# A second Strassen level inside one product of a cross network, with one-bank PSUM tiles and hand-set engine orders, on one NeuronCore

## The chip, the cores and the metric

The kernel runs on one NeuronCore of a Trainium2 chip. The metric is the device time of one execution in microseconds (us), as a median of several runs. A profile is one execution; its span is some 1.7 us shorter than the time reported for the same run. Engines are named as in the profile: PE is TensorE's matmuls, PEld its weight loads, DVE is VectorE, ACT is ScalarE, POOL is GpSimd, SP issues the transfers.

## The reference

```python
B, Din, L = 16384, 1024, 6          # x0 [B, Din], ws [L, Din, Din], bs [L, Din], all bf16
def reference(x0, ws, bs):
    x = x0
    for l in range(L):
        proj = jnp.einsum('bd,de->be', x, ws[l]) + bs[l]
        x = x0 * proj + x
    return x
```

## The kernel before

The batch is cut into 16 pairs of two blocks of 512 rows. A pair goes through 6 layers, so the program is 96 layers one after the other, each needing the result of the one before. Activations lie transposed, `[128, 2, 8, 512]`.

A layer is a 2x2 block product, done with seven products in place of eight (Strassen's scheme in Winograd's form). Each product is 16 matmuls of 128x512. Three things surround the products: VectorE builds four operand differences T1 to T4; ScalarE evicts PSUM (the memory in which TensorE's results land) to bf16 tiles in SBUF, the memory that VectorE works in; VectorE adds the parts, multiplies by x0 and adds x, which gives the next layer's input. Four of the seven weight operands are sums of weight blocks ("combinations"). They are the same for every pair, so VectorE builds those of layer l+1 while pair 0 runs layer l, saves them to DRAM (`Lc`), and later pairs load them.

```python
def emit_T(xsrc, which):                       # T1 = B12-B11, T2 = B22-T1, T3 = B22-B12, T4 = B21-T2
    ...
            nc.vector.tensor_tensor(out=t_[:], in0=B12, in1=B11, op=SUB)
def emit_combo(l, pid):                        # pair 0 only; 5: W12+W22, 6: c5-W11, 3: W21-c6, 7: W11-W12
    ...
    pending_saves.append((l, pid, t_))
def product(pid, pts, start):                  # 16 matmuls into two 2-bank PSUM tiles
    for m in range(KH):
        for k in range(KH):
            nc.tensor.matmul(pts[m // 2][:, m % 2, :], lhsT=wt[:, k, m * P:(m + 1) * P], rhs=rhs[:, k, :], ...)
...
product(1, pA, True);  P1s = evac(pA)
product(5, pX, True);  P5s = evac(pX)
product(3, pX, False); S53 = evac(pX, bias_eh=0)
product(2, pX2, True); P2s = evac(pX2, bias_eh=0)       # product 2 is W21*B21
nc.vector.tensor_tensor(out=C1[:, :, 0, :], in0=P1s, in1=P2s, op=ADD)
final(C1, 0, 0)                                         # c *= x0; x_next = c + x
if combos_next:
    emit_combo(l + 1, 5)
product(6, pA, False); ...; emit_combo(l + 1, 6)
product(7, pA, False); ...; emit_combo(l + 1, 3)
product(4, pA, False); ...; emit_combo(l + 1, 7)
```

A scheduler decides each engine's order within the data dependences.

## Time and profile before

| | before |
|---|---|
| time, median | 2353.59 us (three runs, 2353.52 to 2353.95) |
| PE, DVE, ACT busy | 98%, 73%, 66% of 2352.8 us |
| one steady layer on PE | 24.17 us |
| first matmul starts | 12.63 us |
| from the end of the last layer on PE to the end | 16.0 us |

Two lines of the page of before: the busy time of each engine, and the shares of the chain of work that ended last.

```profile
PE 2312.4 (98%) x10537; PEld 1052.7 (45%) x10752; DVE 1708.6 (73%) x1464; ACT 1556.7 (66%) x2113; POOL 1.2 (0%) x5
...
PE 96%; DVE 1%; DMA 1%; issue 1%; SPq 1%; ACT 0%; another core or an unknown queue 0%; DVEq 0%
```

TensorE is the bound. The next lines are the timeline of PE in before: start, duration, and a run of equal matmuls. Two products that open a layer are shown; no idle time is printed before either.

```profile
1031.43 3.62 PE L196 MATMUL pa<-x0T,wp 128*128 128x512 bf16 x16
...
1055.60 3.62 PE L196 MATMUL pa<-xst,wp 128*128 128x512 bf16 x16
```

The starts are 24.17 us apart for 112 matmuls, 215.8 ns each. (A few matmul records are missing from such traces; the starts are what to use.)

The windows view gives the busy time of each engine in a stretch, here one stretch for each of a few layers of before and one for the end.

```profile
core 0: us, PE busy (x) PEld busy (x) DVE busy (x) ACT busy (x) POOL busy (x), PEclk, DMA share, GB/s
12.63:39.44 26.81, 26.70 (x111) 11.57 (x113) 15.82 (x14) 14.94 (x20) 0.96 (x1) 1.00 0.80 263
39.44:64.05 24.61, 24.22 (x111) 10.97 (x112) 21.78 (x20) 16.21 (x22) 0.00 (x0) 1.00 0.48 156
...
1079.78:1103.95 24.17, 24.07 (x112) 10.97 (x113) 17.56 (x16) 16.20 (x22) 0.00 (x0) 1.00 0.76 263
...
2336.80:2352.80 16.00, 0.15 (x1) 0.00 (x0) 4.50 (x4) 1.27 (x2) 0.00 (x0) 0.57 0.91 227
```

(The DMA share can pass 1.00.) In an ordinary layer (third line) VectorE is busy 17.6 of 24.17 us. In pair 0 it also builds combinations and is busy 21.8 (second line), still less than PE. The last line is the end: VectorE works 4.5 us after the last matmul, then transposes and stores follow.

This is the timeline of DVE in before.

```profile
1046.74 1.22 DVE L235 TENSOR_TENSOR cb<-ev 128x2048 bf16<-128x2048 bf16 x1 [7.94 <-ACT ev L208]
1048.00 1.22 DVE L214 TENSOR_TENSOR cb<-cb,x0T 128x2048 bf16<-128x2048 bf16 x1
1049.26 1.22 DVE L223 TENSOR_TENSOR xst<-cb,x0T 128x2048 bf16<-128x2048 bf16 x1
1050.40 1.22 DVE L241 TENSOR_TENSOR cb<-ev 128x2048 bf16<-128x2048 bf16 x1
```

Each takes 1.22 us. One that needs the result of the one before starts 1.26 us after it; an independent one 1.14 us after it. The bracket on the first line is a wait of 7.94 us, nearly all of VectorE's spare time in that layer.

### The profile page before, as it was taken

Reading aid. Unit: us, or ns where it says so; the run is one execution under the profiler, and the core shown is the slowest. Engines: PE = TensorE matmul, PEld = TensorE weight load, DVE = VectorE, ACT = ScalarE, POOL = GpSimd, SP = SyncE. Lnnn points to the kernel's source line nnn. Section 1 sums busy time; section 2 is a strip of 40 time slices with the busy share of each in tenths; the row PEclk is TensorE's granted clock in tenths of the full one; section 3 lists DMA queues with packets and bytes.
Section 4 is the critical chain, followed back from the end, with each engine's and each line's share of the span. In section 5 each row is a group of like instructions: output and inputs, shape, how many; then the busy total and the mean of one; then the engine's idle time right before and its main releaser. Section 6 shows DMA issues by size and latency. Waiting matters only on the chain.

```text
span 2352.8 us, 27562 instructions
## 1 busy us (share of the span) xinstructions
PE 2312.4 (98%) x10537; PEld 1052.7 (45%) x10752; DVE 1708.6 (73%) x1464; ACT 1556.7 (66%) x2113; POOL 1.2 (0%) x5
## 2 busy tenths in 40 slices
PE   7999999999999999999999999999999999999997
PEld 3444444444444444444444444444444444444443
DVE  5977767676777767676776767677776767777675
ACT  4666666666666666666666666666666666666665
POOL 0000000000000000000000000000000000000000
PEclk9999999999999999999999999999999999999998
DMA  7769485584956849568494774947749476594843
GB/s 226 203 210 256 152 216 196 161 253 154 228 184 171 241 154 240 171 177 235 153 259 153 178 233 152 259 152 190 221 152 260 153 198 214 155 257 152 226 153 86
DMA packets 599987, 457.96 MB, mean 195 GB/s; under 512 B 398128, under 2 KB 550704, under 8 KB 599856
## 3 DMA queue, kind: packets, MB, share of 16 engines
q1 hardware_dynamic: 599856, 456.20, 67.0%
q8 instruction: 85, 1.39, 0.2%
q14 instruction: 46, 0.38, 0.1%
HBM read 342.88 MB, written 46.14 MB: 165 GB/s over the span
## 4 chain that ended last, share of the span: by engine, by line
PE 96%; DVE 1%; DMA 1%; issue 1%; SPq 1%; ACT 0%; another core or an unknown queue 0%; DVEq 0%
PE pa L196 54%; PE px L196 42%; SPq L145 1%; DMA w_313<-in_ws_dram 0%; DMA wp<-in_ws_dram 0%; DVE cb L214 0%; DVE xst L219 0%; DVE xst L223 0%; ACT ev L208 0%; DVE cb L241 0%; DVE cb L250 0%; DVE cb L235 0%; DVE wp L128 0%; DVE T_247 L93 0%; DVE T_811 L93 0%
## 5 line engine op out<-in xcount | busy, mean ns | idle before, releaser
L196 PEld LDWEIGHTS <-wp 128*128 128x128 bf16 x10752 | 1052.7, 98 | 1283.8 <-issue 12.7
L208 ACT ACTIVATE ev<-px,b_all 128x512 bf16<-128x512 f32 x768 | 486.3, 684 | 201.3 <-PE px L196 193.3
L196 PE MATMUL px<-xst,wp 128*128 128x512 bf16 x2510 | 562.5, 379 | 2.7
L235 DVE TENSOR_TENSOR cb<-ev 128x2048 bf16<-128x2048 bf16 x96 | 117.6, 1225 | 594.2 <-ACT ev L208 594.2
L205 ACT CAST ev<-pa 128x1024 bf16<-128x1024 f32 x384 | 388.6, 1012 | 240.2 <-PE pa L196 230.8
L214 DVE TENSOR_TENSOR cb<-cb,x0T 128x2048 bf16<-128x2048 bf16 x384 | 467.8, 1221 | 6.3
L223 DVE TENSOR_TENSOR xst<-cb,xst 128x2048 bf16<-128x2048 bf16 x316 | 385.0, 1222 | 14.5
L208 ACT ACTIVATE ev<-pa,b_all 128x512 bf16<-128x512 f32 x384 | 243.1, 684 | 112.9 <-PE pa L196 108.2
L208 ACT ACTIVATE cb<-pa,b_all 128x512 bf16<-128x512 f32 x384 | 243.1, 684 | 88.4 <-ACT ev L208 48.4
L196 PE MATMUL pa<-xst,wp 128*128 128x512 bf16 x1254 | 287.3, 379 | 1.3
L205 ACT CAST ev<-px 128x1024 bf16<-128x1024 f32 x192 | 194.3, 1012 | 138.1 <-PE px L196 133.1
L241 DVE TENSOR_TENSOR cb<-ev 128x2048 bf16<-128x2048 bf16 x96 | 117.0, 1219 | 0.0
L250 DVE TENSOR_TENSOR cb<-ev 128x2048 bf16<-128x2048 bf16 x96 | 117.0, 1218 | 0.0
L196 PE MATMUL px<-x0T,wp 128*128 128x512 bf16 x501 | 112.4, 379 | 0.5
L223 DVE TENSOR_TENSOR xst<-cb,x0T 128x2048 bf16<-128x2048 bf16 x64 | 78.3, 1223 | 1.5
L196 PE MATMUL pa<-x0T,wp 128*128 128x512 bf16 x251 | 60.2, 391 | 12.9 <-DMA x0T<-in_x_dram 12.6
L130 DVE TENSOR_TENSOR wp<-wp 128x2048 bf16<-128x2048 bf16 x6 | 7.3, 1219 | 2.1 <-DMA wp<-in_ws_dram 2.1
L128 DVE TENSOR_TENSOR wp<-wp 128x2048 bf16<-128x2048 bf16 x6 | 7.3, 1219 | 0.0
L126 DVE TENSOR_TENSOR wp<-w_90,wp 128x2048 bf16<-128x2048 bf16 x1 | 1.2, 1226 | 8.2 <-DMA wp<-in_ws_dram 8.2
L93 DVE TENSOR_TENSOR T_111<-x0T 128x2048 bf16<-128x2048 bf16 x1 | 1.2, 1226 | 5.7 <-DMA x0T<-in_x_dram 5.7
L219 DVE TENSOR_TENSOR xst<-cb,xst 128x2048 bf16<-128x2048 bf16 x4 | 4.9, 1225 | 0.1
L196 PE MATMUL px<-T_247,wp 128*128 128x512 bf16 x16 | 3.6, 378 | 0.3 <-DVE T_247 L93 0.3
(783 smaller groups left out, 1858.9 us busy)
## 6 DMA issues: line engine op xcount, KB each, us to landing
wp<-Lc SPq DMA_DIRECT2D x360, 512.0 KB, 3.4
wp<-in_ws_dram SPq DMA_DIRECT2D x288, 512.0 KB, 3.7
out_dram<-x0T SPq DMA_DIRECT2D x30, 1024.0 KB, 9.8
Lc<-wp SPq DMA_DIRECT2D x24, 512.0 KB, 3.1
out_dram<-xoS SPq DMA_DIRECT2D x4, 512.0 KB, 4.7
w_90<-in_ws_dram SPq DMA_DIRECT2D x1, 512.0 KB, 4.7
x0T<-in_x_dram SPq DMA_TRANSPOSE x32, 7.3
w_130<-in_ws_dram SPq DMA_DIRECT2D x1, 512.0 KB, 5.0
```

What stands on the lines that cost most here:

```text
L128: nc.vector.tensor_tensor(out=t_[:], in0=wtiles[(0, l, 5)][:], in1=W11[:], op=SUB)
L130: nc.vector.tensor_tensor(out=t_[:], in0=W21[:], in1=wtiles[(0, l, 6)][:], op=SUB)
L145: nc.sync.dma_start_transpose(out=x0T_next[:, n], in_=x0[n * NB:(n + 1) * NB, :])
L196: nc.tensor.matmul(pts[m // 2][:, m % 2, :], lhsT=wt[:, k, m * P:(m + 1) * P], rhs=rhs[:, k, :], start=(start and k == 0), stop=(k == KH - ...
L205: nc.scalar.copy(out=dst[:, 2 * h:2 * h + 2, :], in_=pts[h][:])
L208: nc.scalar.activation(out=dst[:, m, :], in_=pts[m // 2][:, m % 2, :], func=IDENT, bias=bias_col(bias_eh, m), scale=1.0)
L214: nc.vector.tensor_tensor(out=c, in0=c, in1=blk(x0T, eh, n), op=MULT)
L219: nc.vector.tensor_tensor(out=xo_last["xfin"][:, eh, n].rearrange("r j k p -> r k j p"), in0=v4(c), in1=v4(blk(xsrc, eh, n)), op=ADD)
L223: nc.vector.tensor_tensor(out=blk(xst, eh, n), in0=c, in1=blk(xsrc, eh, n), op=ADD)
L235: nc.vector.tensor_tensor(out=C1[:, :, 0, :], in0=P1s, in1=P2s, op=ADD)
L241: nc.vector.tensor_tensor(out=C1[:, :, 1, :], in0=U2s, in1=S53, op=ADD)
L250: nc.vector.tensor_tensor(out=C2[:, :, 1, :], in0=U3s, in1=P5s, op=ADD)
```

## The change

The intent is to apply the same scheme once more to one of the seven products, W21*B21 (product 2), so that its 16 matmuls of 128x512 become 7 inner products of four matmuls of 128x256, the work of 14. That needs four inner operands (`emit_t`), three inner sums of 128x512 on VectorE, and a fifth combination per layer, "2i". PSUM tiles become single banks, evicted one by one. The program order is declared binding for TensorE, ScalarE and VectorE. All five combinations of the next layer are now emitted together, in front of the first inner sum. The diff, cut to its core:

```diff
-    psA = ctx.enter_context(tc.tile_pool(name="psA", bufs=2, space=bass.MemoryType.PSUM))
...
+    wring = ctx.enter_context(tc.tile_pool(name="wring", bufs=14))
+    psum = ctx.enter_context(tc.tile_pool(name="ps", bufs=1, space=bass.MemoryType.PSUM))
+    pA = [psum.tile([P, NB], FP32, name=f"pA{i}") for i in range(KH)]
+    pX = [psum.tile([P, NB], FP32, name=f"pX{i}") for i in range(KH)]
+    def emit_t(B):                            # inner operands of 128x512
+        tt(t1, q(0, 1), q(0, 0), SUB); tt(t2, q(1, 1), t1, SUB)      # (joined here)
+        tt(t3, q(1, 1), q(0, 1), SUB); tt(t4, q(1, 0), t2, SUB)
...
+            s = inner_w(t_)                   # the fifth combination, "2i"
+            tt(s[5], a21, a22, ADD)
+            tt(s[6], s[5], a11, SUB)
+            tt(s[3], a12, s[6], SUB)
+            tt(s[7], a11, a21, SUB)
...
+    order_ctx = ctx.enter_context(tc.manual_schedule(engines={nc.tensor.engine, nc.scalar.engine, nc.vector.engine}))
...
     prefetch_upto(PREF)
     flush_saves()
...
+            if combos_next:
+                for pid in (5, 6, 3, "2i", 7):
+                    emit_combo(l + 1, pid)
+            inner(1, 0, True)
+            ev(i15[:, 0, :], pX[0][:])
+            inner(5, 1, True)
+            ...
+            inner(2, 2, True)
+            ev(i2[:], pX[2][:])
+            tt(cq(0, 0), q3(i15[:, 0, :]), q3(i2[:]), ADD)
+            ...                               # groups of products 6 and 7 between inner 6, 3, 7, 4
+            tt(Q2[:], Q2[:], P1s[:], ADD)
+            final(Q2[:], 0, 0)
+            final(U2s[:], 0, 1, mult=False)
+            if not last_layer:
+                emit_T(xst, Tn, (1,))
+            ...                               # rest of product 7, then product 4
+            final(C21[:], 1, 0)
+            if not last_layer:
+                ti_next = emit_t(blk(xst, 1, 0))
+                emit_T(xst, Tn, (2, 3, 4))
```

## The prediction

> **What bounds the kernel now.** TensorE. The page's busy table has PE 98% of 2352.8 us, VectorE (DVE) 73%, ScalarE (ACT) 66%; the chain that ended last is 96% PE. In the timeline 16 matmuls of 128x512 start every 3.4525 us, 215.8 ns each, so a layer's 112 take 24.17 us, and 96 layers 2320 us. The rest, 33 us, is the start (first matmul at 12.6 us, then cold ones, about 3.7 us lost) and the end (about 16 us after the last matmul).
>
> **Per layer.**
> - PE: one 16-matmul product (W21*B21) becomes seven inner products of four 128x256 matmuls. The Trainium skill (TensorE: Matmul & The Clock Gate, "Back-to-back issue gap") gives N/2.4 + 2.5 ns; that agrees with the 215.8 ns here and gives 109.2 ns for N=256, an estimate; the trace of before has no such matmul. 96 x 215.8 + 28 x 109.5 ns = 23.78 us, saving 0.39 us a layer, 37 us in all (1.6%). The weight loads (98 ns in the page) must hide behind 107 ns; I expect they just do.
> - DVE: 15 full 128x2048 ops stay (1.22 us; start to start 1.14 us independent, 1.26 us dependent, from the timeline). Added are 4 inner operand subtractions and 3 inner sums of 128x512, about 0.42 us each (estimate: same slope, and the fixed part of about 150 cycles of VectorE: DVE Perf Modes, "Side-by-side"). DVE goes from about 17.1 to 21 of 23.8 us.
> - ACT: 31 evictions of one bank instead of 22; biased 0.684 us as before, plain about 0.585 us (estimate from 1.012 us for 1024 columns). About 19 us of 23.8: not binding; its one-bank tiles come free before PE needs them.
> - DMA: one weight more per layer, share about 67% to 74%. Not binding.
>
> **Steady layers (pairs 1 to 15).** I added these durations along the fixed orders. The last inner product ends about 18.6 us after the layer's start; its eviction and three dependent DVE ops give the next layer's first operand about 0.3 us before PE asks for it; T2 for product 6 comes equally tight. So PE stays gapless at 23.78 us, but without reserve.
>
> **Pair 0.** DVE also builds next-layer weight combinations, five now, all put before the first inner sum: 4 x 1.2 + 4 x 0.4 us, so DVE needs 27 us per layer and becomes the bound: 26.98 us in layers 1 to 4. In layer 0 they also wait for W22 of layer 1, whose load now stands behind five saves in the queue: about 6 us lost. Together about 19 us of the 37 are given back.
>
> **End.** The last region follows the last product at once; perhaps 1.5 us saved.
>
> **Sum.** 2353.6 - 37 + 19 - 1.5, about 2334 us. Range 2318 to 2350. Chances: faster by over 2% 0.03, within 2% 0.92, slower by over 2% 0.05.
>
> **What would show it.** Windows of 23.78 us per layer in later pairs; 128x256 matmuls 109 to 110 ns apart; PE waits on DVE tiles (xst, T) of about 3 us per layer in pair 0, longest in layer 0 after a DVE wait for weight DMA; DVE busy 86 to 90%; small DVE ops 0.42 us.
>
> **What would make it wrong.** Weight loads not hidden behind 107 ns of streaming: 5 ns per small matmul is 13 us. The eviction-to-sum chain longer than I added up: stalls in every layer, and 0.25 us each cancels the rest of the gain. Small DVE ops nearer 0.5 us: pair 0 and the layer boundaries slip. Combinations fitting into DVE idle time better than I think: towards 2315 us. Weight transfers late at pair boundaries, where DMA is already saturated.

## The result

| | before | after |
|---|---|---|
| median | 2353.69 us | 2344.47 us |
| range | 2353.52 to 2353.95 (4 runs) | 2342.43 to 2346.23 (4 runs) |
| ratio, 95% interval | | 0.996 (0.9946 to 0.9974) |

A ratio is the mean time of one kernel's runs over the mean of the other's in the same rounds, so it is not quite the ratio of the medians. The kernel gains 9.2 us, clear of noise; 19.6 were forecast. The result passed the comparison with the reference.

The same two lines of the page, after.

```profile
PE 2277.5 (97%) x11668; PEld 1164.1 (50%) x11904; DVE 2003.2 (86%) x2160; ACT 1818.9 (78%) x2977; POOL 1.1 (0%) x5
...
PE 87%; DVE 10%; issue 1%; ACT 1%; SPq 1%; DMA 0%; DVEq 0%
```

VectorE has gone from 1% to 10% of the chain that ended last. First a steady stretch, the timeline of PE after: the openings of two layers, and a pair of inner products between them.

```profile
1015.86 1.03 PE L233 MATMUL pA_88<-xst,wp 128*128 128x512 bf16 x4
...
1026.22 0.60 PE L245 MATMUL pX_92<-xst,wp 128*128 128x256 bf16 x4
1026.66 0.60 PE L245 MATMUL pX_93<-ti,wp 128*128 128x256 bf16 x4
...
1039.64 1.03 PE L233 MATMUL pA_88<-x0T,wp 128*128 128x512 bf16 x4
```

The steady layer is 23.78 us, as forecast, and the four small matmuls take 0.44 us. The layer's total says it more exactly: (23.78 us - 96 x 215.8 ns) / 28 = 109 ns each. The weight loads hide. So the loss is not in the steady layers. The windows view after, layer by layer (layers 0, 1, 2 and 5 of pair 0, then a steady layer, the last layer, and the end):

```profile
core 0: us, PE busy (x) PEld busy (x) DVE busy (x) ACT busy (x) POOL busy (x), PEclk, DMA share, GB/s
11.80:49.19 37.39, 26.00 (x123) 12.55 (x125) 24.62 (x32) 19.49 (x32) 0.94 (x1) 0.88 0.90 282
49.19:76.25 27.06, 26.01 (x122) 12.55 (x125) 26.51 (x31) 18.94 (x31) 0.00 (x0) 0.92 0.52 181
76.25:103.46 27.21, 23.78 (x121) 12.05 (x125) 26.52 (x31) 18.94 (x31) 0.00 (x0) 1.00 0.54 151
158.22:183.68 25.46, 25.36 (x122) 12.50 (x125) 23.18 (x28) 18.23 (x30) 0.00 (x0) 0.93 0.57 198
...
1063.42:1087.20 23.78, 23.62 (x123) 12.11 (x125) 20.48 (x23) 18.94 (x32) 0.00 (x0) 1.00 1.12 237
2300.32:2324.10 23.78, 23.62 (x122) 12.02 (x123) 20.62 (x23) 18.95 (x32) 0.00 (x0) 1.00 0.01 1
2324.10:2342.70 18.60, 0.16 (x1) 0.00 (x0) 6.78 (x6) 0.71 (x2) 0.00 (x0) 0.58 0.94 226
```

Compare VectorE (the third busy figure) with the length of the stretch. In the steady layer it is busy 20.5 of 23.78 us. In layers 1 and 2 it is busy 26.5 of 27.1: it is full, and TensorE waits for it. Layer 0 is 11.4 us longer than TensorE is busy in it (37.39 against 26.00), and the end is 18.6 us where it was 16.0.

The differences of the two profiles add up to the whole gain (10.1 us between these two executions, 9.2 between the medians):

| stretch | before | after | difference |
|---|---|---|---|
| up to the first matmul | 12.63 | 11.80 | -0.8 |
| six layers of pair 0 | 148.6 | 171.9 | +23.3 |
| the other 90 layers | 2175.6 | 2140.4 | -35.2 |
| end | 16.0 | 18.6 | +2.6 |
| span | 2352.8 | 2342.7 | -10.1 |

So the second level gains 35 us in pairs 1 to 15, and two thirds of that are given back in pair 0. The six layers there took 37.39, 27.06, 27.21, 27.20, 27.56 and 25.46 us. Against TensorE's own work (23.78 us a layer, plus the 3.5 us that before loses there too, most of it in its first 16 matmuls, which took 6.25 us where later ones took 3.62: 148.6 - 6 x 24.17) that is a loss of 25.7 us: 10.1, 3.3, 3.4, 3.4, 3.8 and 1.7.

The loss in layer 0 shows in VectorE's timeline after: the operation at 26.61 is the last of the set-up, the one at 35.33 the first combination of layer 1.

```profile
26.61 1.22 DVE L91 TENSOR_TENSOR T_137<-x0T,T_131 128x2048 bf16<-128x2048 bf16 x1
35.33 1.23 DVE L91 TENSOR_TENSOR wp<-w_151,wp 128x2048 bf16<-128x2048 bf16 x1 [7.50 <-DMA wp<-in_ws_dram]
36.59 4.07 DVE L91 TENSOR_TENSOR wp<-wp 128x2048 bf16<-128x2048 bf16 x6
```

It waits 7.50 us for a weight block, and everything behind it in the binding order waits as well, the first inner sum included. The transfer queue of after says why the block is late: five saves, which need VectorE's own results, are issued before the loads of W21 and W22.

```profile
17.12 9.92 SPq L126 DMA_DIRECT2D Lc<-wp  x5
27.10 1.34 SPq L83 DMA_DIRECT2D wp<-in_ws_dram  x2
```

Before had this order in its queue too (four saves, then the two loads at 22.49), but there VectorE used W22 only at 32.98, behind work of the layer itself.

On TensorE (timeline after) the openings of the next layers wait for `xst`, VectorE's output:

```profile
49.19 1.87 PE L233 MATMUL pA_88<-xst,wp 128*128 128x512 bf16 x4 [11.28 <-DVE xst L91]
...
76.25 1.02 PE L233 MATMUL pA_88<-xst,wp 128*128 128x512 bf16 x4 [0.95 <-DVE xst L91]
...
103.46 1.02 PE L233 MATMUL pA_88<-xst,wp 128*128 128x512 bf16 x4 [3.27 <-DVE xst L91]
```

The first four matmuls after the 11.28 us of waiting take 1.87 us, the next openings 1.02. The windows view of after around the opening of layer 1 and of layer 5, the PEclk column:

```profile
49.20:52.60 3.40, 3.40 (x9) 1.17 (x10) 3.34 (x3) 0.69 (x1) 0.00 (x0) 0.50 0.68 255
158.22:161.60 3.38, 3.38 (x11) 1.31 (x12) 3.35 (x3) 1.37 (x2) 0.00 (x0) 0.68 1.05 405
```

The clock was 0.50 after 11.28 us of idle time and 0.68 after 3.62 us, as a mean of 3.38 us (in the first 0.98 of these it was still 1.00, in the next 3.30 it was 0.54); after 3.27 us (layers 3 and 4) it stayed at 1.00. In layer 1 this costs nothing, because VectorE is the bound there: the layer takes 27.06 us, layer 2 with the clock at 1.00 takes 27.21. In layer 5, where VectorE has no combinations to build, it makes 1.7 us. The Trainium skill (TensorE: Matmul & The Clock Gate, "The HAM clock gate") has the clock fall to a half after an idle window of about 3.4 us. The half (0.50) agrees, but the length is no sharp limit in these runs: in the run loads_first, told below, the clock fell after 2.89 us before layer 1 (0.50) and after 3.28 us before layer 3 (0.54).

### The profile page after: what moved, and what is told of

Read it like the earlier page. It is cut to its first block, busy times and chain, and to the rows that moved or that the text cites. A ratio compares the mean times of both kernels' runs of the same rounds, so it can differ in the third digit from the quotient of the medians.

```text
span 2342.7 us, 31963 instructions
## 1 busy us (share of the span) xinstructions
PE 2277.5 (97%) x11668; PEld 1164.1 (50%) x11904; DVE 2003.2 (86%) x2160; ACT 1818.9 (78%) x2977; POOL 1.1 (0%) x5
## 4 chain that ended last, share of the span: by engine, by line
PE 87%; DVE 10%; issue 1%; ACT 1%; SPq 1%; DMA 0%; DVEq 0%
PE pA_91 L233 13%; PE pA_88 L233 13%; PE pA_89 L233 13%; PE pA_90 L233 12%; PE pX_92 L245 7%; PE pX_94 L233 6%; PE pX_93 L233 6%; PE pX_95 L233 6%; PE pX_92 L233 6%; DVE ev L91 4%; PE pX_93 L245 3%; DVE xst L91 2%; PE pX_94 L245 2%; DVE wp L91 1%; DVE ti L91 1%
## 5 line engine op out<-in xcount | busy, mean ns | idle before, releaser
L233 PEld LDWEIGHTS <-wp 128*128 128x128 bf16 x9216 | 901.4, 98 | 1026.5 <-issue 55.1
L91 DVE TENSOR_TENSOR ev<-ev,x0T 128x2048 bf16<-128x2048 bf16 x384 | 469.8, 1223 | 9.9
L91 DVE TENSOR_TENSOR xst<-ev,xst 128x2048 bf16<-128x2048 bf16 x320 | 384.9, 1224 | 21.7 <-DVE ev L91 0.5
L91 DVE TENSOR_TENSOR ev<-ev 128x2048 bf16<-128x2048 bf16 x288 | 352.2, 1223 | 38.0 <-ACT ev L249 25.7
L245 PEld LDWEIGHTS <-wp 128*128 128x128 bf16 x2688 | 262.7, 98 | 133.2
L252 ACT ACTIVATE ev<-pA_88,b_all 128x512 bf16<-128x512 f32 x288 | 198.4, 689 | 69.9 <-PE pA_88 L233 65.7
L252 ACT ACTIVATE ev<-pA_90,b_all 128x512 bf16<-128x512 f32 x288 | 198.1, 688 | 34.9 <-PE pA_90 L233 33.4
L252 ACT ACTIVATE ev<-pA_91,b_all 128x512 bf16<-128x512 f32 x288 | 197.9, 687 | 34.0 <-PE pA_91 L233 34.0
L252 ACT ACTIVATE ev<-pA_89,b_all 128x512 bf16<-128x512 f32 x288 | 198.3, 689 | 25.6 <-PE pA_89 L233 1.8
L245 PE MATMUL pX_92<-ti,wp 128*128 128x256 bf16 x1152 | 172.8, 273 | 1.1
L249 ACT CAST ev<-pX_92 128x512 bf16<-128x512 f32 x192 | 112.3, 585 | 28.8 <-PE pX_92 L233 16.7
L233 PE MATMUL pA_88<-xst,wp 128*128 128x512 bf16 x320 | 83.0, 382 | 22.4 <-DVE xst L91 22.4
L252 ACT ACTIVATE ev<-pX_92,b_all 128x512 bf16<-128x512 f32 x96 | 66.0, 687 | 26.6 <-PE pX_92 L233 24.3
L233 PE MATMUL pA_89<-xst,wp 128*128 128x512 bf16 x314 | 83.2, 385 | 0.3
L233 PE MATMUL pA_91<-xst,wp 128*128 128x512 bf16 x315 | 82.3, 381 | 0.6
L233 PE MATMUL pX_94<-xst,wp 128*128 128x512 bf16 x320 | 82.1, 379 | 0.3
L233 PE MATMUL pA_90<-xst,wp 128*128 128x512 bf16 x306 | 81.7, 385 | 0.4
L233 PE MATMUL pX_93<-xst,wp 128*128 128x512 bf16 x308 | 80.5, 379 | 0.7
L233 PE MATMUL pX_95<-xst,wp 128*128 128x512 bf16 x308 | 80.5, 379 | 0.3
L233 PE MATMUL pX_92<-xst,wp 128*128 128x512 bf16 x306 | 80.3, 379 | 0.4
L252 ACT ACTIVATE ev<-pX_93,b_all 128x512 bf16<-128x512 f32 x96 | 66.0, 687 | 16.9 <-PE pX_93 L233 15.7
L252 ACT ACTIVATE ev<-pX_94,b_all 128x512 bf16<-128x512 f32 x96 | 66.0, 687 | 16.9 <-PE pX_94 L233 16.9
```

Of the source, the lines that this page charges most:

```text
L91: nc.vector.tensor_tensor(out=out, in0=in0, in1=in1, op=op)
L233: nc.tensor.matmul(dst[m][:], lhsT=wt[:, k, m * P:(m + 1) * P], rhs=rhs[:, k, :], start=(start and k == 0), stop=(k == KH - 1), skip_group ...
L245: nc.tensor.matmul(dst[:, m * NQ:(m + 1) * NQ], lhsT=wv[:, k, m * P:(m + 1) * P], rhs=ti[i][:, k, :], start=(start and m == 0 and k == 0), ...
L249: nc.scalar.copy(out=dst, in_=src)
L252: nc.scalar.activation(out=dst, in_=src, func=IDENT, bias=bias_col(eh, m), scale=1.0)
```

## The experiments

Theory A: what stretches pair 0 is the volume of VectorE's work, about 27 us a layer once it also builds five combinations, and in layer 0 the wait for W22 behind the saves. Theory B: the place of the combinations in front of the first inner sum delays the chain. Theory C: the inner products, evictions or transfers themselves are slower than thought. Eight kernels were run, five rounds each, in two calls; the runs of before there gave 2354.08 and 2353.88 us.

| run | median us | ratio to before (95%) | result |
|---|---|---|---|
| after | 2344.47 | 0.996 (0.9946 to 0.9974) | correct |
| loads_first | 2337.2 | 0.9929 (0.9915 to 0.9942) | correct |
| spread | 2339.93 | 0.994 (0.9927 to 0.9952) | correct |
| no_combos | 2318.19 | 0.9849 (0.9836 to 0.9862) | wrong weights |
| plain_all | 2361.39 | 1.0033 (1.002 to 1.0046) | correct |
| plain_pair0 | 2329.85 | 0.9898 (0.9883 to 0.9913) | correct |
| plain_last | 2341.2 | 0.9946 (0.9933 to 0.9958) | correct |
| pool | 2416.31 | 1.0264 (1.025 to 1.0278) | correct |
| best | 2319.81 | 0.9855 (0.9841 to 0.9868) | correct |

### loads_first: the loads of layer 1 ahead of the saves

```diff
-    prefetch_upto(PREF)
+    load_w12(1)
+    prefetch_upto(key_pos[(0, 1, 4)] + 1)
     flush_saves()
```

> Only the order of transfers at the start changes: the three weight blocks of layer 1 are loaded ahead of the five saves of layer 0's combinations. Theory A (in layer 0 VectorE waits for W22 of layer 1, 7.5 us in the profile, because its load stands behind the saves in the queue): that wait goes, layer 0 of pair 0 shrinks from 37.4 to about 29.5 us, and the run takes about 2336 us against 2344.5. Rival (the transfer rate of the start itself is the limit, not the order): the wait stays above 4 us and the time stays above 2341.

Measured: 2337.2 us. The windows view of loads_first, layer 0, layer 1, and the openings of layers 1, 3 and 5:

```profile
12.20:41.80 29.60, 26.61 (x122) 12.72 (x124) 24.53 (x32) 19.71 (x32) 0.94 (x1) 1.00 0.85 272
41.80:68.87 27.07, 25.48 (x123) 12.44 (x125) 26.52 (x31) 18.96 (x31) 0.00 (x0) 0.94 0.75 274
41.80:42.80 1.00, 1.00 (x3) 0.40 (x4) 0.99 (x1) 0.00 (x0) 0.00 (x0) 0.50 1.10 414
96.08:99.50 3.42, 3.42 (x9) 1.25 (x10) 3.35 (x3) 0.74 (x2) 0.00 (x0) 0.54 1.25 273
150.51:154.00 3.49, 3.49 (x10) 1.33 (x11) 3.42 (x4) 0.99 (x2) 0.00 (x0) 0.57 1.05 381
```

Layer 0 fell from 37.39 to 29.60 us, to the tenth as expected, and VectorE's waits for weights, 16.0 us in three waits in the changed kernel, are down to 8.9 us in two, both in the set-up. The order in the queue cost 7.8 us; the rate of the transfers did not set this wait. Layers 1 to 4 are as they were: 27.07, 27.21, 27.22 and 27.21. Layer 5 is again 25.46, with a clock of 0.57 at its opening after 3.28 us of idle time.

### spread: the same combinations, in other places

```diff
             if combos_next:
-                for pid in (5, 6, 3, "2i", 7):
-                    emit_combo(l + 1, pid)
...
+    emit_combo(l + 1, 5)          # after T1
+    emit_combo(l + 1, 6)          # these two after the final of block (1, 1)
+    emit_combo(l + 1, 3)
+    emit_combo(l + 1, "2i")       # after T2
+    emit_combo(l + 1, 7)          # after T3
```

> The weight combinations of the next layer are moved from in front of the first inner sum to places spread over the end of the layer; VectorE's work is the same. Theory A (the volume of VectorE work, about 27 us a layer with combinations, is what stretches pair 0): the layers after the first still take about 27 us, now layers 1 to 5; only layer 0 gets shorter, since its combinations come after W22 has landed: about 2335 us. Theory B (their place in front of the sums delays the chain): layers 1 to 5 fall to about 24 us, and the run takes about 2320 us.

Measured: 2339.93 us. Layers 0 to 5 took 25.87, 27.86, 28.07, 28.13, 28.12 and 28.07 us. Here is layer 3 of spread in the windows view:

```profile
94.09:122.22 28.13, 25.54 (x124) 12.40 (x125) 26.62 (x31) 18.97 (x32) 0.00 (x0) 0.94 0.85 249
```

Theory B falls: the layers did not drop to 24 us, VectorE is busy 26.6 us wherever the combinations stand. They even got 0.9 us longer than in the changed kernel, which is where the expectation of 2335 was missed by 5 us: TensorE now also waits for the combinations themselves (its weight loads waited 16.2 us in ten waits on VectorE's `wp`). For these layers the place chosen by the change was the better one; that spread is still 4.5 us faster as a whole comes from layer 0, which no longer waits for W22 (25.87 us against 37.39).

### no_combos: no combinations after layer 0

```diff
+        if l > 0:
+            wtiles[(0, l, pid)] = wtiles[(0, l, RAW[pid])]     # a raw block in place of the combination
+            return
         w12 = load_w12(l)
...
-        return Lc[l, CIDX[pid]].rearrange("p (k e) -> p k e", k=KH)
+        return w_src(l, RAW[pid])
```

> Wrong result on purpose: from layer 1 on no combination is computed or saved; the products use raw weight blocks in their place, and later pairs load raw blocks. Theories A and B: pair 0 runs at 23.8 us a layer from layer 1 on, layer 0 at 27.4, and the run takes about 2318 us, some 26 less than the changed kernel. If the loss lay in the inner products or in the eviction order instead (theory C), layers 1 to 4 would stay above 25 us and the time above 2330.

Measured: 2318.19 us. The comparison with the reference passed although the weights are wrong, so it cannot tell right weights from wrong ones here; a pass there is no proof of arithmetic in this case, and for the other kernels the argument is that they compute the same sums. The windows view of no_combos, layers 0 and 1:

```profile
11.78:37.74 25.96, 25.57 (x122) 12.54 (x124) 18.71 (x24) 18.79 (x31) 0.94 (x1) 1.00 1.08 292
37.74:61.52 23.78, 23.67 (x124) 12.15 (x124) 20.48 (x23) 18.95 (x32) 0.00 (x0) 1.00 0.66 183
```

Without combinations (and their saves, and with them the wait for W22) pair 0 runs at TensorE's pace. The six layers take 145.2 us, 26.7 less than in the changed kernel, and that is the whole difference of the medians (26.3). Theory C falls for pair 0, except for its transfers: the saves and some loads went with the combinations, so this run alone does not separate them from VectorE's work. plain_pair0 does.

### plain_all: no second level, everything else kept

```diff
+            if flat:                                   # flat in every layer
+                for m in range(KH):
+                    group(2, pX, m, True)              # W21*B21 as one product of 16 matmuls
+                    ev(Q2[:, m, :], pX[m][:])
+                tt(Q2[:], Q2[:], P1s[:], ADD)
+                final(Q2[:], 0, 0)
+                ...                                    # products 6 and 7, their sums as before
+            else:
                 inner(1, 0, True)
                 ...
```

> The second level is undone in every layer (one product of 16 matmuls for W21*B21 again, in one-bank tiles), while the hand-set order, the one-bank PSUM tiles, the larger pools, the fifth combination and its load stay. If the second level is all that gains in the steady layers, they take 24.17 us as before, pair 0 about 24.5, and the run about 2354 us, the time of before. If the order and the one-bank tiles gain by themselves, it is under 2348; if they cost, over 2360.

Measured: 2361.39 us, 7 more than expected. The windows view of plain_all, layer 0 and a steady layer:

```profile
12.08:43.83 31.75, 26.18 (x110) 11.12 (x112) 19.74 (x23) 18.59 (x29) 0.93 (x1) 0.98 0.92 294
...
1002.00:1026.17 24.17, 24.07 (x112) 10.93 (x113) 18.97 (x16) 18.03 (x29) 0.00 (x0) 1.00 0.52 175
```

The steady layer is 24.17 us, exactly that of before: the hand-set order and the one-bank tiles gain and lose nothing there, and all 0.39 us per layer come from the second level. The 7.3 us by which it is slower than before are in the first two layers, 31.75 and 26.97 us against 26.81 and 24.61 in before. I had left out that the wait for W22 stays in this kernel (6.28 us in its VectorE timeline), and the cold clock after it (0.50 in the first 3.4 us of layer 1), which here counts because TensorE is the bound.

### plain_pair0: no second level in layers 0 to 4 of pair 0

The same edit with `flat` true for `pr == 0 and l < L - 1`. The five combinations are still built and saved.

> The second level is left out in layers 0 to 4 of pair 0 only; there W21*B21 is one product again, all five combinations are still built and saved. Theory A (volume of VectorE work): VectorE needs about 24.4 us in such a layer, TensorE 24.17, so layers 2 to 4 take 24.2 to 24.8 us instead of 27.2; layers 0 and 1 as in the run with no second level at all, about 31.8 and 27.0 (the wait for W22 and the cold clock after it stay); the run takes about 2333 us, 11 to 12 less than the changed kernel. Rival (the transfers of pair 0, not VectorE, set its pace): layers 2 to 4 stay above 26 us, time above 2341.

Measured: 2329.85 us, 14.6 below the changed kernel, 3 better than expected. The layers took 31.86, 26.47, 24.22, 24.62, 24.62 and 25.06 us. The windows view of plain_pair0, layer 2:

```profile
70.32:94.54 24.22, 24.11 (x111) 10.88 (x112) 23.20 (x24) 18.06 (x29) 0.00 (x0) 1.00 0.58 175
```

Taking 2.9 us of work off VectorE per layer (seven instructions of 0.42 us) and giving 0.39 us to TensorE turned 27.2 us into 24.2 to 24.6. That is theory A, from the other side: the transfers are the same.

### plain_last: the last layer of the last pair

The same edit with `flat` true for that one layer.

> Only the last layer of the last pair goes back to one product for W21*B21. Theory A (the longer end, 18.6 us after the last matmul against about 16, is VectorE's backlog, 6.7 us of work after the last matmul against 4.7): TensorE takes 0.4 us more, VectorE ends about 4.2 us after the last matmul, and the run gains 1.5 to 2.5 us: about 2342.5. Rival (the transposes and stores themselves got slower): no gain, and the end stays above 18 us.

Measured: 2341.2 us. The runs scatter by more than the effect (2339.35 to 2343.86 here, 2342.43 to 2346.23 for after), so the profile decides. The windows view of plain_last, last layer and end:

```profile
2302.52:2326.69 24.17, 24.02 (x110) 10.84 (x111) 20.86 (x18) 18.05 (x29) 0.00 (x0) 1.00 0.16 31
2326.69:2342.10 15.41, 0.00 (x0) 0.00 (x0) 3.84 (x4) 0.72 (x2) 0.00 (x0) 0.57 0.89 226
```

From the start of the last layer to the end it is 39.6 us, against 42.4 after and 40.2 before. VectorE has 3.8 us of work left after the last matmul where it had 6.8, and from its last operation to the end it is 11.5 us (2330.6 to 2342.1) against 11.7 (2331.0 to 2342.7) after and 11.4 before. So the longer end was VectorE's backlog, not the transposes or stores.

### pool: combinations on GpSimd

```diff
+        eng = nc.gpsimd if l > 0 else nc.vector
-            tt(t_[:], w12[:], W22[:], ADD)
+            tt(t_[:], w12[:], W22[:], ADD, eng)          # and so for all five; loads first as above
```

> The five combinations of layers 1 to 5 are computed on the idle GpSimd engine, with the weight loads of layer 1 ahead of the saves; VectorE keeps only the layer's own work. Theory A: if GpSimd takes no more than about 20 us for the five and does not slow VectorE, pair 0 runs at 23.8 us a layer and the run takes 2318 to 2322 us. If it is slower than a layer or slows VectorE down, pair 0 stays above 27 us a layer and the run above 2335; either way its own durations show which.

Measured: 2416.31 us; layers 0 to 4 took 40 to 48 us. The timelines of POOL and of DVE in this run, at the same moment:

```profile
51.65 5.02 POOL L91 TENSOR_TENSOR wp<-w,wp 128x2048 bf16<-128x2048 bf16 x1
...
52.80 9.95 DVE L91 TENSOR_TENSOR xst<-ev,x0T 128x2048 bf16<-128x2048 bf16 x2
62.85 4.88 DVE L91 TENSOR_TENSOR T<-xst 128x2048 bf16<-128x2048 bf16 x1
67.66 2.17 DVE L91 TENSOR_TENSOR ev<-ev 128x2048 bf16<-128x2048 bf16 x1
```

Of the 36 VectorE instructions of 128x2048 that overlap GpSimd's combinations in this trace, 31 took 1.57 to 5.09 us and five the usual 1.22; the 1408 others took 1.21 to 1.24. An idle engine is not a free engine. The Trainium skill (SBUF — State Buffer, "SBUF: two separate sides") says that GpSimd and a VectorE instruction with two SBUF inputs take one shared port pair by turns, whole instructions at a time. The durations here agree with that: the VectorE instruction at 50.71 (2.05 us) ends 1.1 us after the GpSimd instruction at 49.56 (2.13 us) that it overlaps, close to the 1.22 us that it takes alone.

### best: three edits together

Loads first, plain product in layers 0 to 4 of pair 0 and in the very last layer.

> Loads of layer 1 ahead of the saves, no second level in layers 0 to 4 of pair 0 and in the very last layer. The gains should add: layer 0 about 27.8 us, layers 1 to 4 about 24.4, the rest 23.78, the end about 2 us shorter: about 2325 us, which beats both kernels (2344.5 and 2353.7). If the parts overlap instead of adding, above 2331.

Measured: 2319.81 us, ratio 0.9855, which beats both kernels: 1.45% under before. The windows view of best, layers 0 and 1 and the end:

```profile
11.79:38.41 26.62, 26.51 (x110) 11.51 (x112) 21.08 (x24) 17.89 (x28) 0.94 (x1) 1.00 0.97 303
38.41:62.70 24.29, 24.18 (x111) 10.89 (x112) 23.88 (x24) 18.06 (x29) 0.00 (x0) 1.00 0.74 259
...
2302.34:2317.70 15.36, 0.17 (x1) 0.00 (x0) 3.84 (x4) 0.72 (x2) 0.00 (x0) 0.65 0.90 227
```

The six layers of pair 0 take 149.6 us (171.9 after). With no long idle time left, the clock stays at 1.00. It came out 5 us better than the 2325 expected, but the parts of that expectation had been summed wrongly: 27.8 + 4 x 24.4 + 23.8 is 149.2 us for pair 0, and 2344.5 - (171.9 - 149.2) - 2 is 2320. The parts themselves were close: layer 0 took 26.6, layers 1 to 4 took 24.3 to 24.6, layer 5 took 25.06, and the end is 3.2 us shorter. Its runs lie within 0.5 us of one another (2319.5 to 2319.94), where the changed kernel's scatter over 4. What makes that scatter was not tested; in the profile of plain_last layer 5, the same work, took 26.53 us against 25.46, with the clock at 0.56 for its first 6.38 us.

## Why the prediction was right or wrong

The forecast was 2334 us, the result 2344.47. The gain of the second level and what eats it in pair 0 were foretold rightly, but the losses were 10 us short: of 37 us gained, the forecast gave back 19 in pair 0 and counted 1.5 at the end as a gain. Three steps failed: the end (a gain of 1.5 us, measured a loss of 2.6), the term for layer 0 ("about 6 us lost", measured 10.1), and layer 5, for which no loss was counted (measured 1.7).

- **Steady layers: right.** 23.78 us were forecast and measured. The 109.2 ns estimate for a 128x256 matmul, from the Trainium skill (TensorE: Matmul & The Clock Gate, "Back-to-back issue gap"), met 109; the weight loads hide. The small VectorE instructions take 0.42 us as estimated, the plain evictions 0.585. The plain_all run shows that the gain is the second level's alone.
- **Pair 0, layers 1 to 4: right.** 26.98 us were forecast, 27.06 to 27.56 measured. The cause was shown from two sides, by taking away the combinations (no_combos: 23.77 to 24.15) and by taking away the second level (plain_pair0: 24.2 to 24.6 in layers 2 to 4), and the rival of position fell with spread.
- **Pair 0, layer 0: mechanism right, size wrong.** "about 6 us lost" was 10.1. That VectorE would wait for W22 behind the five saves was right. TensorE's wait at the end of layer 0 is 11.28 us in the changed kernel and 2.89 in loads_first. The 2.89 are what the combinations' work leaves, near the 3.2 us forecast for the other layers; the other 8.4 are the order in the queue (7.8 in the length of the layer, since the first matmuls of loads_first were 0.6 us slower). The loss above is 10.1 and not 11.3, because it grants the start 3.5 us, of which the changed kernel's first 16 matmuls took only 2.2. If the 6 us were meant to hold the 3.2 of work too, some 3 us were left for a wait that measured 7.50. The block was issued at 27.6, once the last save had its operand, and landed 7.7 us later, where the median of such loads in before is 3.7.
- **Pair 0, layer 5: left out.** 1.7 us. TensorE waits over 3 us for VectorE before it, and its clock falls. The prediction reckoned the waits, but not what they do to the clock afterwards. (Without them the layer gains less than 1.7: in best, with the clock at 1.00, it takes 25.06.)
- **The end: wrong.** "The last region follows the last product at once; perhaps 1.5 us saved" was the step that failed: the end is 2.6 us longer. The binding order leaves VectorE five full instructions to start after the last matmul (two in before), since the second, third and fourth regions of the output (its four blocks) come late and close together: 6.8 us of work, where before has 4.5. The last region cannot follow the last product at once, because VectorE is still at the two before it. plain_last, with 3.8 us of work left, takes the loss away. The prediction itself had called VectorE's chain at the end of a layer "without reserve".

Together: pair 0 lost 25.7 us where 19 were forecast (6.7 more), the end moved by +2.6 where -1.5 was forecast (4.1 more), and the first matmul came 0.8 us sooner, which makes the 10 us between forecast and result.

The remaining 1.3 us in layer 5 of plain_pair0 and best are VectorE's backlog too: in best VectorE runs without a gap from layer 4 into layer 5, and TensorE's products on T1, xst and T2 begin about 0.05 us after VectorE has written them, 0.15, 0.28 and 0.85 us late by their starts.

What stays open: why the loaded queue took 7.7 us for that block in particular (the sharing with the saves is argued, the order is shown).

## What to carry to other kernels

Taking work off the bounding engine moves the bound: add up every other engine's work per stage, not per run, for an average of 86% can hide a stage at 98% and one that pays a one-time cost. With binding in-order queues, one operand that comes late holds up everything behind it, so put loads that the critical engine needs soon ahead of saves that nobody waits for, and use the cheaper form of an algorithm only in the stages where the other engines have room for it. A wait of some 3 us on TensorE can also have a second cost, a colder clock (here after 2.89, 3.28 and 3.62 us, though twice not after 3.27), which counts only if TensorE is the bound afterwards.

## What the Trainium skill lacked or had wrong

- TensorE: Matmul & The Clock Gate, "Back-to-back issue gap", gives about 131 ns per matmul of N=512 as a sustained rate of load and matmul pairs. Here such pairs run at 215.8 ns each for a whole run (16 in 3.4525 us), which is that section's formula for the isolated gap; the formula also held for N=256 (109 ns). (Elsewhere the page has 215.7 ns for back-to-back matmuls, which these runs bear out.)
- VectorE: DVE Perf Modes has the duration right (1.22 us for 2048 bf16 columns) but gives no start-to-start time for a dependent and an independent instruction; the traces show 1.26 and 1.14 us, 10% apart, which a sum for a stage that VectorE fills has to use.
- GPSIMD Engine Reference, "Elementwise — side-by-side cycle accounting", has 4497 ns for an fp32 `tensor_tensor` of 2048 columns and none for bf16: in the pool run it took 4.5 to 4.8 us (means by group) beside a working VectorE, with any waiting inside, so no gain from bf16 is seen; bf16 without VectorE beside it was not measured. That section says nothing of what VectorE loses at that time: 1.22 us became up to 5.09 us.
- No page gives a landing time for a load that stands behind saves in the same queue: 7.7 us for 512 KB here, against a median of 3.7 us in before.
